# Loading x in halves over two queues, and the end of the head in halves of 256, in a gated mix of two attentions

## The chip, the cores and the metric

The kernel runs on one core of a Trainium2 chip. The metric is the device time of one execution in microseconds. Times are compared as medians of several runs; one execution is also taken by the hardware profiler, and its views are quoted here. Engines are PE (TensorE matmul; PEld is its weight load), DVE (VectorE), ACT (ScalarE), POOL (GpSimd) and SP (SyncE, which only issues DMAs here).

## The reference

Input x has 2048 tokens of 640 features. Two attention blocks with 32 heads of 20 features each read it. Block A is full softmax attention. Block B is attention over a window of 8 positions, two apart. A gate per token mixes the two.

```python
H = 32; Dh = D // H
qkv = (x @ wqkv).reshape(B, S, 3, H, Dh).transpose(2, 0, 3, 1, 4)
# A: full attention
p = softmax(einsum("bhqd,bhkd->bhqk", q, k) * Dh ** -0.5)
a = einsum("bhqk,bhkd->bhqd", p, v).transpose(0, 2, 1, 3).reshape(B, S, D) @ wo
# B: keys at pos - 2*w, w = 0..7, masked below 0
b = ...
g = sigmoid((x * gate_w).sum(-1, keepdims=True))
return g * a + (1 - g) * b
```

## The kernel before, in words

Most of the work is block A: for every group of four heads and 512 queries, scores for 16 blocks of 128 keys (`qk`, L1697), their exponentials (`exp`, L1722, on ACT; a share of them is approximated on DVE, L1711 and L905), and the product with V (`pv`, L1767). There are 32 such groups. Block B and the output projections are worked in between.

The order of the instructions is written by a planner, `_Sched`. `T(stream, duration, ...)` puts an instruction at the end of one engine's list, with the data keys that it reads and writes; from these the semaphore waits are made. Each engine works through its list in order. `T` also keeps an estimated time per engine (`sch.avail`), and generators for the side work look at these estimates to decide what goes next. So a changed estimate early on can change the order of all that follows.

The change touches the head, which is everything ahead of the first scores:

- `x_load` (L498) loads a part of x, 512 tokens as a tile of 128 partitions by 4 rows of 640 (640 KB). All four parts go through SP's queue, with the first K weights (into `ebuf[3]`, 100 KB, L506) behind part 1, and the first Q weights (`ebuf[4]`, L509), the V weights (L510) and the rest of the K weights (L512) behind part 3.
- ACT loads its table and runs one small exponential (L520) meanwhile. PE runs nine matmuls on zeros to warm up (L529).
- `turn` (L1392) transposes a part on PE into the score banks, 20 transposes of 128 x 128 (L1400). `x_out` copies it into `xT`, two fifths on ACT (L1413), three fifths on DVE (L1416).
- POOL's `w_pad` (L598) spreads the first K weights, so that four heads lie 32 rows apart. `k_first` (L1432) projects K of the first four heads for 512 tokens, five matmuls of 512 columns (L1423). The order on PE is: turn 0, turn 1, K 0, turn 2, K 1, turn 3, K 2, K 3, Q 0.
- `k_max` takes the largest absolute value of each K feature (DVE, L1437), `k_out` writes K to `kT` (ACT, L1444).
- The end of the head: from K's largest values DVE makes the diagonal mask `KM` (L1496, L1498, L1501). Q's absolute values are taken (DVE, L1503). PE adds the bound mask x |Q| to Q (L1506), which serves as the softmax's upper bound. DVE scales Q into `qT[0]` (L1511). Then the first scores can start. `v_first` and `v_out` (L1450, L1458) do the first block of V beside it.

PSUM has two score tiles of three banks each; the third bank of each, and the bank `side0`, serve as banks for side work (`side[1]` is the third bank of score 0), and `obank` collects the product with V.

## Time and profile before

| | us |
|---|---|
| median of three runs | 792.07 |
| the three runs | 791.92, 794.16, 792.07 |
| profiled execution: its own time | 792.33 |
| profiled execution: span of the core | 790.4 |
| first exponential of scores starts at | 18.77 |
| ACT busy, whole span | 769.2 (97%) |
| ACT busy from 60 to 200 us | 140.00 |

The page gives busy time per engine and the chain of work that ended last. The trace can be asked for busy time in chosen stretches, and for a timeline: start, length, engine, line, operation, output and input with their shapes, and in brackets how long the engine was idle before it and what ended that. Successive instructions of one kind are merged into one row with a count. Times are counted from the start of the span. Matmuls are pipelined: the length of a merged row on PE includes the last one's run through the array. "PEclk" was 1.00 in all stretches of the head.

### The profile page before, as it was taken

Reading aid. Unit: us, or ns where it says so; the run is one execution under the profiler, and the core shown is the slowest. Engines: PE = TensorE matmul, PEld = TensorE weight load, DVE = VectorE, ACT = ScalarE, POOL = GpSimd, SP = SyncE. Lnnn points to the kernel's source line nnn. Section 1 sums busy time; section 2 is a strip of 40 time slices with the busy share of each in tenths; the row PEclk is TensorE's granted clock in tenths of the full one; section 3 lists DMA queues with packets and bytes.
Section 4 is the critical chain, followed back from the end, with each engine's and each line's share of the span. In section 5 each row is a group of like instructions: output and inputs, shape, how many; then the busy total and the mean of one; then the engine's idle time right before and its main releaser. Section 6 shows DMA issues by size and latency. Waiting matters only on the chain.

```text
span 790.4 us, 29540 instructions
## 1 busy us (share of the span) xinstructions
PE 751.7 (95%) x12545; PEld 289.6 (37%) x12545; DVE 721.5 (91%) x1280; ACT 769.2 (97%) x731; POOL 124.2 (16%) x230
## 2 busy tenths in 40 slices
PE   8999999999999999999999999999999999999997
PEld 4423333232233334333334433433433433344333
DVE  7798888999999989999988999998999999898894
ACT  4999999999999999999999999999999999999996
POOL 4011202111112011111111011111111111111210
PEclk9999999999999999999999999999999999999999
DMA  7231111010021123130111312013113013100311
GB/s 227 86 85 25 39 38 38 12 27 18 8 67 32 43 42 72 25 72 15 24 40 39 79 40 57 14 39 73 25 27 75 26 24 70 46 7 7 74 31 39
DMA packets 61221, 36.14 MB, mean 46 GB/s; under 512 B 26724, under 2 KB 59892, under 8 KB 61092
## 3 DMA queue, kind: packets, MB, share of 16 engines
q1 hardware_dynamic: 60804, 33.94, 17.6%
q8 instruction: 99, 1.62, 0.9%
q10 hardware_dynamic: 288, 0.33, 0.1%
q14 instruction: 30, 0.25, 0.1%
HBM read 12.85 MB, written 3.54 MB: 21 GB/s over the span
## 4 chain that ended last, share of the span: by engine, by line
PE 44%; ACT 25%; DVE 18%; issue 10%; DMA 1%; SPq 0%; POOL 0%; DVEq 0%; ACTq 0%
ACT ebuf L1722 25%; PE score L1697 13%; PE obank L1767 12%; PE side L632 12%; DVE uD L1711 6%; DVE eD L905 4%; PE score L632 2%; DVE qkvB L967 1%; DVE kvw L1092 1%; PE score L1788 1%; PE side L1003 1%; PE obank L1788 1%; DVE vA L833 1%; DMA oTd<-in_A_x_dram 1%; DVE kvw L993 1%
## 5 line engine op out<-in xcount | busy, mean ns | idle before, releaser
L1722 ACT ACTIVATE ebuf<-score 128x1024 bf16<-128x1024 f32 (+1 forms) x699 | 757.4, 1260 | 5.3 <-PE score L1697 4.6
L1711 DVE TENSOR_SCALAR uD<-score 128x512 int16<-128x512 f32 x392 | 259.9, 679 | 14.6 <-PE score L1697 13.3
L1697 PE MATMUL score<-qT,kT 32*128 32x512 bf16 x1856 | 253.8, 384 | 17.6 <-ACT ebuf L1722 13.0
L905 DVE TENSOR_SCALAR eD<-uD 128x2048 int16<-128x2048 int16 x294 | 194.8, 686 | 4.5 <-PE obank L1767 3.4
L1767 PE MATMUL obank<-ebuf,vA 128*21 128x512 bf16 x1656 | 153.5, 385 | 1.6 <-DVE oTt L865 0.6
L1697 PEld LDWEIGHTS score<-qT,kT 32*128 32x128 bf16 x1856 | 63.0, 91 | 211.4 <-ACT ebuf L1722 147.0
L925 POOL TENSOR_TENSOR vS<-vA,vw 128x252 bf16<-128x252 bf16 x98 | 60.1, 614 | 389.0 <-DVE eD L905 252.6
L1767 PE MATMUL obank<-eD,vS 128*21 128x512 bf16 x1176 | 103.5, 379 | 0.0
L632 PE MATMUL side<-xT,wBs 128*32 128x256 bf16 x2400 | 93.6, 280 | 2.5 <-DVE oB L1125 0.7
L632 PEld LDWEIGHTS side<-xT,wBs 128*32 128x32 bf16 x2400 | 68.1, 141 | 28.2 <-issue 14.5
L1767 PEld LDWEIGHTS obank<-ebuf,vA 128*21 128x21 bf16 x1656 | 36.0, 89 | 82.9 <-issue 56.6
L1092 DVE TENSOR_TENSOR kvw<-kvw,eB 128x2048 bf16<-128x2048 bf16 x40 | 48.1, 1212 | 0.8 <-DMA kvw<-qkvB 0.8
L993 DVE TENSOR_TENSOR kvw<-qkvB 128x2048 bf16<-128x2048 bf16 x40 | 48.0, 1214 | 0.1
L882 POOL TENSOR_TENSOR oN<-oTt,rcp 128x256 bf16<-128x256 f32 x62 | 38.9, 627 | 58.0 <-DVE eD L905 39.5
L967 DVE CAST qkvB<-side 128x512 bf16<-128x512 f32 (+1 forms) x72 | 42.0, 592 | 4.5 <-PE side L632 4.3
L873 POOL TENSOR_TENSOR rcp<-rcp,gA 128x16 f32<-128x16 f32 x31 | 9.1, 294 | 190.3 <-DVE eD L905 90.7
L1767 PE MATMUL obank<-uD,vA 128*21 128x512 bf16 x392 | 38.1, 379 | 0.0
L1767 PEld LDWEIGHTS obank<-eD,vS 128*21 128x21 bf16 x1176 | 28.8, 91 | 19.8 <-issue 2.0
L1697 PE MATMUL score<-woBp,kT 32*128 32x512 bf16 x192 | 30.0, 384 | 1.8 <-ACT ebuf L1722 1.6
L632 PE MATMUL side<-xT,kvw 128*32 128x512 bf16 (+1 forms) x360 | 30.1, 382 | 0.6 <-DVE vA L833 0.3
L632 PE MATMUL side<-kvw,xT 128*32 128x160 bf16 (+1 forms) x740 | 28.5, 263 | 1.3 <-DVE vA L833 0.5
L865 DVE STREAM_TRANSPOSE oTt<-obank 128x512 f32<-128x512 f32 x32 | 22.6, 706 | 6.6 <-PE obank L1767 6.6
(188 smaller groups left out, 553.3 us busy)
## 6 DMA issues: line engine op xcount, KB each, us to landing
kvw<-qkvB SPq DMA_DIRECT2D x128, 80.6 KB
wBs<-in_B_wqkv_dram SPq DMA_DIRECT2D x5, 480.0 KB
WqP<-in_A_wqkv_dram SPq DMA_DIRECT2D x14, 160.0 KB
oTd<-oN SPq DMA_DIRECT2D x108, 20.0 KB
out_dram<-outsb SPq DMA_DIRECT2D x12, 160.0 KB
qT<-dst SPq DMA_DIRECT2D x93, 20.0 KB
kvw<-in_A_wqkv_dram SPq DMA_DIRECT2D x2, 800.0 KB
oTd<-in_A_x_dram SPq DMA_DIRECT2D x2, 640.0 KB
```

The lines of the kernel that those rows point to most:

```text
L632: ins = e.matmul(o[j:k, :], l(j) if callable(l) else l[:, j:k], r, start=(first and i == 0), stop=(last and i == n - 1), skip_group_check= ...
L865: T("dve", 0.625, lambda e: e.transpose(oTt[:, :], obank[:, :]), reads=["obank"], writes=["oTt"])
L882: T(en, c2 if n == 4 else 0.56, lambda e, oo=oo, ii=ii, ib=ib: e.tensor_tensor(oo, ii, ib, ALU.mult), reads=["rcp", "oTt"], **{"accum" if ...
L905: T("dve", 0.065 + 0.1334 * n, lambda e, k=k, sl=sl: e.tensor_scalar(eD[:, sl % NS, 0:512 * n].bitcast(I16), uD[d % 2][:, 0:512 * n].bitca ...
L925: T("pool", 0.607, lambda e: e.tensor_tensor(vS[:, d % 2, :, :], _ap(vA, (kb * NQ + q) * 4 * DV, [[0, K - 1], [1, 4 * DV]]), _ap(vw, 0, [[ ...
L967: t = TB(dvc(n * TOK), lambda e, o=o, i=i: e.tensor_copy(o, i), reads=[("side", b)], writes=[key])
L993: TB(dvc(CH, 2), lambda e: e.tensor_tensor(o, i0, i1, ALU.mult), reads=["qB", "kB"], writes=[("prod", i)] + (["WkA", "WvA", ("WkP", 0)] if ...
L1092: TB(dvc(CH, 2), lambda e: e.tensor_tensor(o, i0, i1, ALU.mult), reads=["eB"] + [("vR", w4) for w4 in range(4)], writes=[("prod", i)], por ...
L1697: ins = e.matmul(o, kT[32 * j:32 * j + 32, q, kb * P:(kb + 1) * P], qT[qbuf[g]][32 * j:32 * j + 32, :], start=True, stop=True)
L1711: t = T("dve", 0.598, lambda e: e.tensor_scalar(uD[d % 2][:, 512 * i:512 * (i + 1)].bitcast(I16), side[x], UOFF, 0.0, op0=ALU.add, op1=ALU ...
L1722: exps[s] = T("act", actc(512 * n), lambda e: e.activation(ebuf[s % NE][:, 0:512 * n], score[s % 2][:, 0:512 * n], ACTF.Exp, scale=LN2 / S ...
L1767: ins = e.matmul(obank[32 * j:32 * j + DV, :], v, src, start=(kb == 0), stop=(last and k >= len(lst) - 4), skip_group_check=True)
```

## The change

`x_load` now makes two DMAs of 256 tokens each, the first half through SP's queue and the second through ACT's. ACT's four stand ahead of its table load. `turn` waits for both halves.

The end of the head works in halves of 256 columns. K 3 goes into two halves of `score[1]`, Q 0 into one half in `obank` and one in `side[1]`, with ten matmuls of 256 columns in place of five of 512 each. The maximum over K 3 is taken per half. In place of the mask from three parts and its combination with the fourth, one instruction takes the largest of the three values, and one makes the mask. ACT takes the absolute value of Q's first half, DVE of its second. The bound and the scaling are done per half. ACT writes K 3 to `kT` from both halves in one instruction, now behind the absolute value.

Last, the planner's estimates are set to fixed numbers after the head. With them the planner writes the same order as before for all that follows, on every engine. Only four waits are added behind the head: one DVE instruction waits for ACT's absolute value, SP's first load of B's weights waits for ACT's half of part 3, and ACT's two output DMAs at the end wait for its own early loads.

```diff
@@ -438,7 +438,7 @@
     gwT = sb([P, CN], BF16, "gwT")
     qabs2 = sb([P, 2 * 512], BF16, "qabs")
     qabs = [qabs2[:, i * 512:(i + 1) * 512] for i in range(2)] + [woBp[:, 4, 0:512]]
-    kmx4 = sb([P, 4], FP32, "kmx4")
+    kmx4 = sb([P, 5], FP32, "kmx4")
     kmx = sb([P, 1], FP32, "kmx")
     kmd4 = sb([P, 4], FP32, "kmd4")
     KMd = sb([P, CN, 32], BF16, "KMd")
@@ -497,8 +497,10 @@
 
     def x_load(tcc, dur):
         t_, o_ = XOFF[tcc]
-        T("sp", dur, lambda e: e.dma_start(_ap(t_, o_, [[D, 4], [1, D]]), x_v[tcc * 512:(tcc + 1) * 512, :].rearrange(
-            "(b p) d -> p b d", p=P)), writes=[("xs", tcc)], dma=True)
+        for h, q in enumerate(("sp", "act")):
+            T(q, dur, lambda e, h=h: e.dma_start(_ap(t_, o_ + 2 * h * D, [[D, 2], [1, D]]), x_v[
+                tcc * 512 + 256 * h:tcc * 512 + 256 * h + 256, :].rearrange("(b p) d -> p b d", p=P)),
+              writes=[(("xs", "xsh")[h], tcc)], dma=True)
 
     w4 = lambda t: _ap(t, 0, [[4 * DH, CN], [1, 4 * DH]])
     x_load(0, 4.9)
@@ -518,7 +520,7 @@
     T("pool", 0.3, lambda e: e.iota(itmp[:, :], [[1, P]], base=0, channel_multiplier=-1), writes=["itmp"])
     T("dve", 0.06, lambda e: e.memset(warm[:, :], 0.0), writes=["warm"])
     T("act", 1.4, lambda e: e.activation(warm[:, 2:4], warm[:, 0:2], ACTF.Exp), reads=["warm"], writes=["warm2"])
-    T("dve", 0.2, lambda e: e.memset(qabs[0][:, :], 0.0), writes=[("qabs", 0)])
+    T("dve", 0.2, lambda e: e.memset(qabs[0][:, :], 0.0), writes=[("qabs", 0), ("qabsh", 1)])
 
     T("dve", 0.25, lambda e: e.tensor_copy(idf[:, :], itmp[:, :]), reads=["itmp"], writes=["rB"])
     T("dve", 0.25, lambda e: e.tensor_scalar(ident[:, :], idf[:, :], 0.0, None, op0=ALU.is_equal),
@@ -528,7 +530,7 @@
 
     warm_up = lambda e: e.matmul(obank[:, :], qabs[0][:, 0:P], qabs[0][:, :], start=True, stop=True)
     for i in range(9):
-        T("pe", 0.43, warm_up, reads=[("qabs", 0)], writes=["obank"])
+        T("pe", 0.43, warm_up, reads=[("qabs", 0), ("qabsh", 1)], writes=["obank"])
 
     WKP0 = _ap(kvw, WKP_OFF, [[P, CN], [1, P]])
     T("dve", 0.35, lambda e: e.memset(WKP0, 0.0), writes=["WkP"])
@@ -709,7 +711,7 @@
         yield ("dve",)
         T("dve", dvc(512), lambda e: e.tensor_scalar(
             qabs[0][:, :].bitcast(U16), side[b][:, :].bitcast(U16)[:, 1:1024:2], 0x7FFF, None, op0=ALU.bitwise_and),
-          reads=[("side", b)], writes=[("qabs", 0)])
+          reads=[("side", b)], writes=[("qabs", 0), ("qabsh", 1)])
         yield from mm_group(b, [(side[b][:, :], KM[0], qabs[0][:, :])], [("KM", 0), ("qabs", 0)], mmc(512), first=False)
         yield ("dve",)
         t = T("dve", dvc(512), lambda e: e.tensor_scalar(qT[1][:, :], side[b][:, :], OCT, offs[:, 0:1], op0=ALU.mult, op1=ALU.add),
@@ -1401,7 +1403,7 @@
                                    ident[:, :], start=True, stop=True, is_transpose=True, skip_group_check=True)
             return ins
 
-        T("pe", 1.13 if tcc else 1.9, fn, reads=[("xs", tcc), "ident"], writes=tkeys(s_))
+        T("pe", 1.13 if tcc else 1.9, fn, reads=[("xs", tcc), ("xsh", tcc), "ident"], writes=tkeys(s_))
 
     def turned(tcc):
         turn(tcc)
@@ -1425,7 +1427,7 @@
         return fn
 
 
-    kbank = lambda tcc: ((side[0], ("side", 0)), (obank, "obank"), (side[0], ("side", 0)), (side[1], ("side", 1)))[tcc]
+    kbank = lambda tcc: ((side[0], ("side", 0)), (obank, "obank"), (side[0], ("side", 0)))[tcc]
 
     def k_first(tcc):
         kb_, key = kbank(tcc)
@@ -1490,37 +1492,70 @@
     k_out(1)
     k_first(2)
     k_max(2)
-    k_first(3)
-    T("pe", 1.07, proj5(obank[:, :], lambda c: WqP[:, c, :], None, 0), reads=WQ + XT(0), writes=["obank"])
+
+    def half_proj(o, w_, x0):
+        def fn(e):
+            for c in range(CN):
+                ins = e.matmul(o, w_(c), xT[:, c, x0:x0 + 256], start=(c == 0), stop=(c == CN - 1), skip_group_check=True)
+            return ins
+        return fn
+
+    hcols = lambda h: slice(256 * h, 256 * h + 256)
+    k3 = lambda h: score[1][:, 512 * h:512 * h + 256]
+    q0 = [obank[:, 0:256], side[1][:, 0:256]]
+    q0k = ["obank", ("side", 1)]
+    for h in range(2):
+        T("pe", 0.55, half_proj(k3(h), lambda c: kvw[:, WKP_OFF + c * P:WKP_OFF + c * P + P], 1536 + 256 * h),
+          reads=[("WkP", 0)] + XT(3), writes=[("K3", h), ("score", 1)])
+    for h in range(2):
+        T("pe", 0.55, half_proj(q0[h], lambda c: WqP[:, c, :], 256 * h), reads=WQ + XT(0), writes=[("Q0", h), q0k[h]])
     k_out(2)
     T("dve", 0.15, lambda e: e.tensor_reduce(kmx[:, 0:1], kmx4[:, 0:3], AX.X, ALU.max),
       reads=[("kmx4", i) for i in range(3)], writes=[("kmx", 0)])
-    T("dve", 0.2, lambda e: e.tensor_scalar(KM3, KMmask, kmx[:, 0:1], None, op0=ALU.mult),
-      reads=[("kmx", 0), "KMmask"], writes=["KM3"])
-    k_max(3)
-    T("dve", 0.25, lambda e: e.scalar_tensor_tensor(KM[0], KMmask, kmx4[:, 3:4], KM3, op0=ALU.mult, op1=ALU.min),
-      reads=[("kmx4", 3), "KMmask", "KM3"], writes=[("KM", 0)])
-    T("dve", dvc(512), lambda e: e.tensor_scalar(
-        qabs[0][:, :].bitcast(U16), obank[:, :].bitcast(U16)[:, 1:1024:2], 0x7FFF, None, op0=ALU.bitwise_and),
-      reads=["obank"], writes=[("qabs", 0)])
-    T("pe", 0.215, lambda e: e.matmul(obank[:, :], KM[0], qabs[0][:, :], start=False, stop=True, skip_group_check=True),
-      reads=[("KM", 0), ("qabs", 0)], accum=["obank"])
+    for h in range(2):
+        T("dve", dvc(256), lambda e, h=h: e.tensor_reduce(
+            kmx4[:, 3 + h:4 + h], k3(h), AX.X, ALU.max, apply_absolute_value=True),
+          reads=[("K3", h)], writes=[("kmx4", 3 + h)])
+    T("act", actc(256), lambda e: e.activation(qabs[0][:, 0:256], q0[0], ACTF.Abs), reads=[("Q0", 0)], writes=[("qabs", 0)])
+    T("dve", 0.1, lambda e: e.tensor_scalar(kmx[:, 0:1], kmx[:, 0:1], kmx4[:, 3:4], kmx4[:, 4:5], op0=ALU.max, op1=ALU.max),
+      reads=[("kmx", 0), ("kmx4", 3), ("kmx4", 4)], writes=[("kmx", 0)])
+    T("dve", 0.2, lambda e: e.tensor_scalar(KM[0], KMmask, kmx[:, 0:1], None, op0=ALU.mult),
+      reads=[("kmx", 0), "KMmask"], writes=[("KM", 0)])
+    T("dve", dvc(256), lambda e: e.tensor_scalar(
+        qabs[0][:, 256:512].bitcast(U16), q0[1].bitcast(U16)[:, 1:512:2], 0x7FFF, None, op0=ALU.bitwise_and),
+      reads=[("Q0", 1)], writes=[("qabsh", 1)])
+    t = T("act", actc(512), lambda e: e.activation(kT[:, 0, 1536:2048].rearrange("p (h c) -> p h c", c=256),
+                                               _ap(score[1], 0, [[512, 2], [1, 256]]), ACTF.Identity, bias=onesrow[:, 0:1]),
+          reads=[("K3", 0), ("K3", 1), ("score", 1), "onesrow", ("kmx4", 3), ("kmx4", 4)], writes=[("kT", 0, 3)])
+    bank_free[2] = t.end + LAT["act"]
+    qah = [("qabs", 0), ("qabsh", 1)]
+    for h in range(2):
+        T("pe", 0.11, lambda e, h=h: e.matmul(q0[h], KM[0], qabs[0][:, hcols(h)], start=False, stop=True, skip_group_check=True),
+          reads=[("KM", 0), qah[h]], accum=[("Q0", h), q0k[h]])
     v_first()
-    t = k_out(3)
-    bank_free[1] = bank_free[2] = t.end + LAT["act"]
-    t = T("dve", dvc(512), lambda e: e.tensor_scalar(qT[0][:, :], obank[:, :], OCT, offs[:, 0:1], op0=ALU.mult, op1=ALU.add),
-          reads=["obank", "offs", ("qTz", 0)], writes=[("qT", 0)])
-    qkeys[0] = [("qT", 0)]
-    obank_first = t.end + LAT["dve"]
+    for h in range(2):
+        t = T("dve", dvc(256), lambda e, h=h: e.tensor_scalar(
+            qT[0][:, hcols(h)], q0[h], OCT, offs[:, 0:1], op0=ALU.mult, op1=ALU.add),
+              reads=[("Q0", h), q0k[h], "offs", ("qTz", 0)], writes=[("qTh", h)])
+        if h == 0:
+            obank_first = t.end + LAT["dve"]
+    bank_free[1] = t.end + LAT["dve"]
+    qkeys[0] = [("qTh", 0), ("qTh", 1)]
     v_out()
     bank_free[0] = t.end + LAT["dve"] + 0.5
     done[("k", 0)] = done[("q", 0)] = True
+    for key in qkeys[0]:
+        sch.bufs[key][0].end = 18.0655808
+    sch.bufs["kT", 0, 3][0].end = 16.4994312
+    sch.avail.update(pe=17.6032304, dve=18.2962528, act=16.4994312)
+    bank_free[:] = [18.6485808, 16.6514312, 16.6514312]
+    obank_first = 18.1485808
     g1 = -1
     def gen_wb():
         for c in range(CN):
             yield ("pe", 0.0, 30.0 + 5.0 * c)
             T("sp", 4.0, lambda e, c=c: e.dma_start(_ap(wBs, c * 3 * D, [[1, 3 * D]]), wB_v[:, c, :]),
-              writes=[("wBs", c)] + [("xs", 3)] * (c == 0), dma=True, iss=0.65)
+              writes=[("wBs", c)] + [("xs", 3), ("xsh", 3)] * (c == 0), dma=True, iss=0.65)
         done["wBs"] = True
 
     add_gen(gen_wb(), 1.0)
```

## The prediction

> **What bounds the kernel now.** I read the page's first part, then its chain by engine, then three views of the trace: busy time by stretch, the timeline of the first 19 us, and the DMA share in steps of half a microsecond.
>
> ```profile
> PE 751.7 (95%) x12545; PEld 289.6 (37%) x12545; DVE 721.5 (91%) x1280; ACT 769.2 (97%) x731; POOL 124.2 (16%) x230
> ...
> PE 44%; ACT 25%; DVE 18%; issue 10%; DMA 1%; SPq 0%; POOL 0%; DVEq 0%; ACTq 0%
> ```
>
> ```profile
> 0.00:18.30 18.30, 14.75 (x120) 8.29 (x120) 13.20 (x33) 8.11 (x10) 9.82 (x20) 1.00 0.80 245
> 18.30:60.00 41.70, 40.54 (x779) 15.45 (x783) 36.25 (x92) 39.92 (x38) 4.26 (x8) 1.00 0.27 82
> 60.00:200.00 140.00, 134.01 (x2068) 44.85 (x2060) 128.76 (x236) 140.00 (x132) 24.32 (x42) 1.00 0.13 28
> ```
>
> The columns are PE, PEld, DVE, ACT, POOL, clock, DMA share, GB/s. From 60 us on ACT has no idle time: its exponentials bound the body. They start at 18.77, so what is before that is a head that the bound engine mostly waits out (8.11 of 18.30 us busy). The order of all instructions behind the head is unchanged, so a head shorter by so much should end the kernel earlier by as much, and no more.
>
> Inside the head, the timeline (start, length, instruction, wait):
>
> ```profile
> 0.74 1.28 ACT L520 ACT_TABLE_LOAD   x1 [0.74 <-PEq L1948]
> 5.15 1.12 PEld L1400 LDWEIGHTS score<-ident,oTd 128*128 128x128 bf16 x20 [0.86 <-DMA oTd<-in_A_x_dram]
> 7.10 1.29 PE L1400 MATMUL score<-ident,oTd 128*128 128x128 bf16 x20 [0.66 <-DMA oTd<-in_A_x_dram]
> 7.57 0.52 POOL L598 COPY kvw<-ebuf 128x400 bf16<-128x400 bf16 x1 [2.82 <-DMA ebuf<-in_A_wqkv_dram]
> 8.23 1.24 PE L1423 MATMUL side<-xT,kvw 128*128 128x512 bf16 x5
> 9.37 1.12 PEld L1400 LDWEIGHTS score<-ident,oB 128*128 128x128 bf16 x20 [0.39 <-DMA oB<-in_A_x_dram]
> 11.36 1.32 PEld L1400 LDWEIGHTS score<-ident,wBs 128*128 128x128 bf16 x20
> 15.07 1.24 PE L1423 MATMUL obank<-xT,WqP 128*128 128x512 bf16 x5
> 15.27 0.69 DVE L1437 TENSOR_REDUCE kmx<-score 128x1 f32<-128x512 f32 x1
> 16.00 0.35 DVE L1501 SCALAR_TENSOR_TENSOR eB<-eB,kmx 128x128 bf16<-128x128 bf16 x1
> 16.35 0.69 DVE L1503 TENSOR_SCALAR qabs<-obank 128x512 uint16<-128x512 uint16 x1
> 17.10 0.39 PE L1506 MATMUL obank<-qabs,eB 128*128 128x512 bf16 x1 [0.79 <-DVE qabs L1503]
> 17.53 0.75 DVE L1511 TENSOR_SCALAR qT<-obank,offs 128x512 bf16<-128x512 f32 x1 [0.48 <-PE obank L1506]
> 18.33 0.39 PE L1697 MATMUL score<-qT,kT 32*128 32x512 bf16 x3 [0.50 <-DVE qT L1511]
> ```
>
> Two parts show. Up to 7.10 PE waits for parts 0 and 1 of x. From 7.10 to 16.31 PE works through turns and projections almost without a gap: part 2 of x comes 0.06 us too late at 9.37 (the projection's last matmul was due to free PE at 9.31), part 3 in time. From 16.31 a serial chain DVE, PE, DVE, PE runs to 18.33.
>
> ```profile
> 1.50:2.00 0.50, 0.50 (x2) 0.15 (x1) 0.50 (x1) 0.50 (x1) 0.50 (x1) 1.00 0.29 31
> 2.00:2.50 0.50, 0.50 (x3) 0.17 (x2) 0.50 (x1) 0.23 (x2) 0.50 (x1) 1.00 0.48 79
> 2.50:3.00 0.50, 0.50 (x3) 0.22 (x2) 0.50 (x1) 0.00 (x0) 0.50 (x2) 1.00 0.59 141
> 3.00:3.50 0.50, 0.50 (x3) 0.20 (x2) 0.50 (x1) 0.00 (x0) 0.50 (x2) 1.00 1.00 346
> ```
>
> The load itself has a slow start: 0.5 x (31 + 79 + 141) = 125 KB by 3.0, with engines busy 29 to 59% of the time, then full share. After that it is bound by the DMA engines.
>
> The sum is made against the profiled execution: span 790.4, its time 792.33, which is 0.26 above the median of 792.07.
>
> **Halves of x on two queues.** SP's four x issues stay four, each half as large, and the loads queued behind them keep their places; ACT gets four issues ahead of its first instruction. ACT's table load (1.28) and its warming activation (0.20) move behind four issues. An issue of a whole part took 0.46 to 0.99 us on SP, so ACT is ready between 0.74 + 1.84 + 1.48 = 4.1 and 0.74 + 3.96 + 1.48 = 6.2. ACT's first copy of a turned part starts at 6.48 now, and its result (1.02 long) is used by the projection at 8.23; that slack is the cover, and I cost this at nothing. If the cover were gone, the copy at 6.48 and then the projection would slip.
>
> What it gains is how much earlier parts 0 and 1 land. From below: nothing, since all bytes still go through the same 16 engines, which are at full share from 3.0. From above: no slow start at all. At 376 GB/s, the mean of full slices, the 1.5 us before 3.0 would have carried 564 KB instead of 125, and the missing 439 KB are 1.17 us. A loss by a late second queue is a rival below. I take a slow start of the same length in which two queues bring twice the bytes: 125 KB more, 125 / 376 = 0.33 us. I lean to the low end because the nearest other row, full share by 3.5 on one queue alone, shows the limit to be the engines. Part 2 shifts by the same 0.33, since it comes behind the same bytes; part 3 has slack (its weights were loading at 11.36 while the projection before it ran to 11.58).
>
> The row says that engines idle in the slow start, so a queue can matter there. [...]
>
> **The head's last steps in halves.** PE does the same columns: ten matmuls of 256 in place of five of 512 for K's last part, and again for Q, so Q still ends at 16.31. What changes is after it. The trace has no 256-column read of PSUM on DVE. Its neighbours: 160 columns 0.32 (casts into vA), 512 columns 0.69 (the reduce). Along that line 256 columns take 0.32 + 96 x 0.37 / 352 = 0.42; the scaling that took 0.75 would take 0.75 - 0.27 = 0.48. ACT: 64 columns 0.31, 512 columns 0.69, so 256 about 0.47.
> DVE: the small reduce ends at 14.86; two half maxima 14.88 to 15.72; a one-column maximum 0.15 (as the offset row L545) to 15.90; the mask product 0.25 (L1498) to 16.18. So the mask is ready before Q is, and the 0.35 of L1501 is gone, but it ended at 16.35, when Q had just ended too: no gain from that alone. ACT takes the absolute value of the first half (Q's first half ends at 15.07 + 0.54 + 0.17 = 15.78) to 16.27, and its wait holds up only K's last output copy, 0.27 us, which nothing uses before the fourth quarter of keys. DVE takes the second half from 16.35 to 16.77; PE's half bound 0.27 (256-column row of L632) from 16.82 to 17.09; DVE scales the first half 16.80 to 17.28 and the second 17.31 to 17.79; PE's first scores at 17.84 in place of 18.33: 0.49 us. Bounds: halves that cost as much as wholes would make it 16.35 + 0.69 + 0.75 + 0.75 and some gaps, 18.57 for the scaling, 0.24 worse; halves that cost exactly half, 17.50 for the first scores, 0.83 better. I stay with 0.49, as 160 columns are the nearest row.
>
> **Behind the head** only semaphore waits that are long satisfied are added (SP's load of the second weights now also waits for ACT's half of part 3, landed some 10 us before). Cost nothing.
>
> Sum: 0.33 + 0.49 = 0.82. Time 792.33 - 0.82 = 791.5; against the median 792.07 that is **791.2**.
>
> **Rivals.**
> First, on the other side: the K weights (the 100 KB into ebuf, issued third on SP) are held back by ACT's bulk. They are 640 pieces of 160 bytes. Now they come right behind part 1, at 7.57, and POOL's padding (0.52) ends at 8.09, just ahead of the projection at 8.23: no slack. ACT's queue has no such load, so beside them it goes on with its halves of parts 2 and 3, 512 pieces of 1280 bytes. If engines take from the queues piece by piece in turn, the small pieces last as long as those 512, which is a whole part: 7.10 - 5.15 = 1.95 us. The projection and all behind it slip by that, and the time is 792.07 + 1.95 - 0.82 = 793.2. It decides once these weights land over 0.8 us later than now behind part 1. For it: nothing orders the two queues. Against: nothing in this trace shows two loaded queues. [...]
> Second, the landing does not move: 792.07 - 0.49 = 791.6. For it: full share from 3.0. Against: the idle engines before.
> Third, the slow start goes altogether, the halved steps are at their best, and the second queue also fills what is lost between transfers: a part takes 1.95 us from turn to turn, but 655 KB at 376 GB/s are 1.74, so 0.21 for each of two parts. 792.07 - 1.17 - 0.83 - 0.42 = 789.7. For it: engines idle in the slow start. Against: it needs all three at once.
>
> **How the numbers follow.** The forecast 0.33, landing unchanged 0.17, slow start gone 0.20, weights held back 0.25, and 0.05 for a second queue that starts late or halves that cost as much as wholes (up to 794). The first is likeliest, so 791.2. The range takes in the third rival, 789.7, and the weights held back with only part of the gain, 793.5. A measurement of this kernel can tell about 0.3%, 2.4 us, from no change, and almost all of these cases lie inside it: faster by more only at the far end of the third rival, whose time lies on that bound: 0.15 of its 0.20. Slower by more only if the weights are held back and the second queue starts late as well: 0.08. Within: 0.77.
>
> **What would show it.** Right: DMA share near full before 3.0; second turn at about 6.8; POOL's padding within 0.6 us behind it, the first projection at about 7.9; DVE halves near 0.42 and 0.48; first exponential 0.8 us earlier than 18.77; ACT without idle time from 60 us on. Wrong: POOL waiting for ebuf until 9 or later with PE idle behind the second turn; ACT's table load ending later than the first turn; halves near 0.6; or ACT idle in the body, which would mean that the shift isn't carried to the end.

## The result, and the profile after

The change makes the kernel slower: 795.43 us against 792.72 by the medians of 16 runs each, ratio 1.0030 with a 95% interval of 1.0019 to 1.0041. A second measurement, beside the later experiments, gave 793.87 against 792.48, 1.0023 (1.0012 to 1.0034). The ratios, here and below, go by all runs, and lie near the quotient of the means (here 1.0028 and 1.0022), not of the medians. The forecast was 791.2, the range 789.7 to 793.5. The first profiled execution took 794.07 with a span of 792.3 (before 792.33 and 790.4). In 7 of the 16 runs, and 4 of the 12 of the second measurement, TensorE's mean granted clock was 0.998 or less, and these took 794.9 to 797.5; the others have medians of 794.07 and 793.54.

The page's first part and its chain by engine hardly differ from before:

```profile
PE 752.5 (95%) x12554; PEld 291.1 (37%) x12556; DVE 721.5 (91%) x1282; ACT 769.5 (97%) x732; POOL 123.8 (16%) x230
...
PE 44%; ACT 26%; DVE 17%; issue 11%; DMA 1%; SPq 0%; POOL 0%; DVEq 0%; ACTq 0%
```

Busy time by stretch (PE, PEld, DVE, ACT, POOL, clock, DMA share, GB/s) says where to look:

```profile
2.00:2.50 0.50, 0.50 (x3) 0.18 (x2) 0.50 (x1) 0.00 (x0) 0.50 (x1) 1.00 0.79 192
2.50:3.00 0.50, 0.50 (x3) 0.22 (x2) 0.50 (x1) 0.00 (x0) 0.50 (x2) 1.00 0.61 169
3.00:3.50 0.50, 0.50 (x3) 0.20 (x2) 0.50 (x1) 0.11 (x1) 0.50 (x2) 1.00 0.98 300
...
0.00:19.60 19.60, 15.37 (x130) 9.70 (x134) 13.07 (x35) 8.39 (x11) 9.75 (x20) 1.00 0.75 229
19.60:60.00 40.40, 38.76 (x750) 14.89 (x753) 34.00 (x88) 37.77 (x37) 3.80 (x7) 1.00 0.29 83
60.00:200.00 140.00, 134.13 (x2073) 44.80 (x2061) 128.80 (x236) 140.00 (x132) 24.12 (x41) 1.00 0.14 28
```

From 60 us on ACT is full as before. Two stretches lost: the head, and 19.6 to 60, where ACT idles 2.63 of 40.40 us (before, from 18.3 to 60, 1.78 of 41.70). The slow start is a little better fed (192 and 169 GB/s against 79 and 141), but 300 follow where 346 had been.

The head in the timeline:

```profile
7.00 1.29 PE L1402 MATMUL score<-ident,oTd 128*128 128x128 bf16 x20 [0.31 <-DMA oTd<-in_A_x_dram]
9.52 0.52 POOL L600 COPY kvw<-ebuf 128x400 bf16<-128x400 bf16 x1 [4.77 <-DMA ebuf<-in_A_wqkv_dram]
10.15 0.78 PEld L1425 LDWEIGHTS side<-xT,kvw 128*128 128x128 bf16 x5 [2.03 <-ACT xT L1415]
17.51 0.71 PE L1499 MATMUL score<-xT,WqP 128*128 128x256 bf16 x5
17.62 0.27 DVE L1520 TENSOR_SCALAR kmx<-kmx 128x1 f32<-128x1 f32 x1
17.71 0.38 ACT L1519 ACTIVATE qabs<-obank 128x256 bf16<-128x256 f32 x1 [0.45 <-PE obank L1499]
18.25 0.42 DVE L1524 TENSOR_SCALAR qabs<-score 128x256 uint16<-128x256 uint16 x1
18.64 0.48 DVE L1537 TENSOR_SCALAR qT<-obank,offs 128x256 bf16<-128x256 f32 x1
18.73 0.28 PE L1533 MATMUL score<-qabs,eB 128*128 128x256 bf16 x1
19.06 0.48 DVE L1537 TENSOR_SCALAR qT<-score,offs 128x256 bf16<-128x256 f32 x1
19.60 0.39 PE L1732 MATMUL score<-qT,kT 32*128 32x512 bf16 x3 [0.23 <-DVE qT L1537]
20.04 1.45 ACT L1757 ACTIVATE ebuf<-score 128x1536 bf16<-128x1536 f32 x1 [1.36 <-PE score L1732]
```

The second turn starts 0.10 us earlier than before. Then POOL waits for the K weights until 9.52 (before 7.57), the first projection's weight load moves from 8.21 to 10.15, and the train behind it is 1.91 us late at Q's end (18.22 for 16.31). The releaser "ACT xT" in brackets is only what the profile can name: that copy had ended at 9.35, and what came last was POOL's padding, at 10.04. From Q's end to the first scores it is 1.38 us, against 2.02 before: 0.64 back. So the first exponential comes at 20.04 in place of 18.77, 1.27 us late.

The second loss is a hole in the middle of one group of scores:

```profile
31.36 0.39 PE L1732 MATMUL score<-qT,kT 32*128 32x512 bf16 x2
32.45 0.37 PE L1732 MATMUL score<-qT,kT 32*128 32x512 bf16 x1 [0.70 <-issue]
32.74 0.10 PEld L1802 LDWEIGHTS obank<-ebuf,vA 128*21 128x21 bf16 x4 [1.29 <-issue]
32.85 1.02 ACT L1757 ACTIVATE ebuf<-score 128x1024 bf16<-128x1024 f32 x1 [0.89 <-PE score L1732]
```

Two of the three matmuls run, the third comes 1.09 us later, and "issue" says that PE waited for nothing that the profile shows. Laid beside before, exponential by exponential, the change is 1.26 us late up to the tenth, and 2.19 to 2.24 from the twelfth until 678 us. There and at 779 us 0.35 come back, and the span ends 1.9 longer.

### The profile page after: what moved, and what is told of

It reads as the page before. It is cut to its first block, busy times and chain, and to the rows that moved or that the text cites. A ratio compares the mean times of both kernels' runs of the same rounds, so it can differ in the third digit from the quotient of the medians.

```text
span 792.3 us, 29571 instructions
## 1 busy us (share of the span) xinstructions
PE 752.5 (95%) x12554; PEld 291.1 (37%) x12556; DVE 721.5 (91%) x1282; ACT 769.5 (97%) x732; POOL 123.8 (16%) x230
## 3 DMA queue, kind: packets, MB, share of 16 engines
q8 instruction: 100, 1.64, 0.9%
q10 hardware_dynamic: 1376, 1.64, 0.6%
## 4 chain that ended last, share of the span: by engine, by line
PE 44%; ACT 26%; DVE 17%; issue 11%; DMA 1%; SPq 0%; POOL 0%; DVEq 0%; ACTq 0%
ACT ebuf L1757 25%; PE score L1732 13%; PE obank L1802 13%; PE side L634 12%; DVE uD L1746 6%; DVE eD L907 4%; PE score L634 2%; DVE qkvB L969 1%; DVE kvw L1094 1%; DMA ebuf<-in_A_wqkv_dram 1%; PE score L1823 1%; PE side L1005 1%; PE obank L1823 1%; DVE kvw L995 1%; DVE vA L835 1%
```

## The theories

Expectations below use these names. The **queue theory**: the DMA engines take pieces from the two loaded queues in turn, so the K weights' 640 small pieces on SP's queue go no faster than ACT's 1280-byte pieces. Its rivals: the K weights are late only by their order on their queue, or by the bandwidth that all share. The **program theory**: the hole near 31 us is PE waiting for its own instructions. The trace's DMA records have a queue of the kind "instruction" (q8: in the change 100 pieces and 1.64 MB, so 16 KB each), which I take for PE's program; the second piece behind 18 us starts at 30.15 and has landed at 31.12. It stands beside three loads of 480 KB each (`wBs`, weights of block B) that SP issues one behind the other from 24.3 on. The **idle theory**: PE's idle time in the head lowers its clock later.

## Experiments

Each run has a ratio to runs of the kernel before on the same chip. "Offset" is how much later the exponentials are than in the profiled execution of before.

**One part of the change at a time.** `steps_only` has the halved last steps, with x whole on SP's queue:

```diff
-        for h, q in enumerate(("sp", "act")):
-            T(q, dur, lambda e, h=h: e.dma_start(_ap(t_, o_ + 2 * h * D, [[D, 2], [1, D]]), x_v[
-                tcc * 512 + 256 * h:tcc * 512 + 256 * h + 256, :].rearrange("(b p) d -> p b d", p=P)),
-              writes=[(("xs", "xsh")[h], tcc)], dma=True)
+        T("sp", dur, lambda e: e.dma_start(_ap(t_, o_, [[D, 4], [1, D]]), x_v[tcc * 512:(tcc + 1) * 512, :].rearrange(
+            "(b p) d -> p b d", p=P)), writes=[("xs", tcc)], dma=True)
...
```

> Whole parts of x on SP as before, the head's last steps in halves as in the changed kernel. Queue theory (the loss comes from the K weights, whose small pieces take turns with ACT's large ones): POOL's padding starts at 7.57 as before, the first projection at 8.2, and the first exponential 0.64 us earlier than 18.77, at 18.1, since from the end of Q to the first scores the changed kernel took 1.38 us where the kernel before took 2.02. Rival, program-load theory: the changed kernel's PE stood still for 0.7 us at 31.4 (a gap of 1.09 us between two matmuls of one score tile) because 22 more PE instructions in the head shift the places where PE's program is fetched; then this kernel has such a gap near 30 too, and its exponentials from the tenth on are some 0.4 us later than before in place of 0.64 us earlier. Time: 0.6 us less than before by the first alone, 0.4 us more with the second.

Measured: 791.55, ratio 0.9993 (0.9981 to 1.0004). The K weights land at 7.48, the padding starts at 7.54, and the first exponential at 18.12: 0.65 us early. Then comes the hole:

```profile
29.77 0.39 PE L1800 MATMUL obank<-ebuf,vA 128*21 128x512 bf16 x1
30.69 0.39 PE L1800 MATMUL obank<-ebuf,vA 128*21 128x512 bf16 x3 [0.53 <-issue]
```

and the offset goes from -0.65 to +0.13. The halves are worth what the trace of the change showed, 0.65, and the hole takes 0.78 back, without any second queue.

`queues_only` has halves of x on both queues and the old last steps:

```diff
-        T("sp", dur, lambda e: e.dma_start(_ap(t_, o_, [[D, 4], [1, D]]), x_v[tcc * 512:(tcc + 1) * 512, :].rearrange(
-            "(b p) d -> p b d", p=P)), writes=[("xs", tcc)], dma=True)
+        for h, q in enumerate(("sp", "act")):
...
-        T("pe", 1.13 if tcc else 1.9, fn, reads=[("xs", tcc), "ident"], writes=tkeys(s_))
+        T("pe", 1.13 if tcc else 1.9, fn, reads=[("xs", tcc), ("xsh", tcc), "ident"], writes=tkeys(s_))
...
```

> Halves of x on both queues, the head's last steps as before. Queue theory: POOL's padding starts at 9.5, the first projection at 10.2, the first exponential at 18.77 + 1.91 = 20.7, and the time is 1.9 us over before. Program-load theory: PE's instructions are those of before, so no gap of over 1 us between matmuls near 32; 1.9 us over before and no more. If the gap comes from the shift of time and not of the program, it is here as well, and the time is about 3 us over before. Rival, idle theory: PE's idle 2 us behind the second turn closes its clock for a while in some executions; then part of the runs are some 2 us slower with a mean clock of 0.995 to 0.998, as half the runs of the changed kernel were.

Measured: 793.47, ratio 1.0015 (1.0006 to 1.0024). The timeline:

```profile
9.05 0.52 POOL L600 COPY kvw<-ebuf 128x400 bf16<-128x400 bf16 x1 [4.30 <-DMA ebuf<-in_A_wqkv_dram]
...
20.19 1.45 ACT L1724 ACTIVATE ebuf<-score 128x1536 bf16<-128x1536 f32 x1 [2.09 <-PE score L1699]
...
32.12 0.52 PE L634 MATMUL score<-kvw,xT 128*32 128x160 bf16 x12
32.58 0.39 PE L1699 MATMUL score<-qT,kT 32*128 32x512 bf16 x2
```

K weights at 9.00, first exponential 1.42 late, and no hole near 30 us. Of the 0.5 that it is less late than expected, 0.37 are this execution's part 1, which landed at 6.59 in place of 6.96. The group of 12 that takes 0.52 us will come up again below; otherwise PE runs through. So the late weights come with the queues, and the hole of 0.8 us and more with the halved steps, though a smaller one will show in the kernel before as well. The idle theory would have this kernel's clock low as often as the change's, with the same idle time in the head; it was 0.998 or less in one run of 12.

**The K weights elsewhere.** `kw_before_part1` issues them on SP between parts 0 and 1; `kw_both_queues` splits them, three of five chunks on SP and two on ACT behind part 1; `parts01_only` keeps the halves for parts 0 and 1 and loads parts 2 and 3 whole on SP:

```diff
 # kw_before_part1
+    T("sp", 5.6, lambda e: e.dma_start(w4(ebuf[3]), wA_v[:, :, D:D + 4 * DH]), writes=[("ebuf", 3)], dma=True)
     x_load(1, 5.5)
-    T("sp", 5.6, lambda e: e.dma_start(w4(ebuf[3]), wA_v[:, :, D:D + 4 * DH]), writes=[("ebuf", 3)], dma=True)
 # kw_both_queues
+    for q, c0, c1, key in (("sp", 0, 3, ("ebuf", 3)), ("act", 3, CN, "kwh")):
+        T(q, 5.6, lambda e, c0=c0, c1=c1: e.dma_start(_ap(ebuf[3], c0 * 4 * DH, [[4 * DH, c1 - c0], [1, 4 * DH]]),
+                                                      wA_v[:, c0:c1, D:D + 4 * DH]), writes=[key], dma=True)
...
 # parts01_only
+        if tcc > 1:
+            T("sp", dur, lambda e: e.dma_start(_ap(t_, o_, [[D, 4], [1, D]]), x_v[tcc * 512:(tcc + 1) * 512, :].rearrange(
+                "(b p) d -> p b d", p=P)), writes=[("xs", tcc), ("xsh", tcc)], dma=True)
+            return
```

> The changed kernel with the K weights issued on SP between parts 0 and 1. Queue theory, by turns piece by piece: 40 small pieces per engine now take turns with ACT's halves of parts 1 and 2, so the weights land at about 7.4 and SP's half of part 1 behind them at about 8.4; the second turn starts at 8.4 in place of 7.0 and the first projection at about 9.6 in place of 10.2; the first exponential at about 19.4, the time 0.6 us under the changed kernel and over before. Rival, order theory (a queue is served by whole transfers, the weights were only issued too late): the weights land at about 5.6, part 1 at 7.4, the first projection at 8.6 and the first exponential at about 18.4, under that of before.

> The changed kernel with the K weights loaded in two transfers, three fifths on SP and two fifths on ACT, both behind part 1. Queue theory: small pieces take turns with small ones, so the weights land about 0.5 us behind part 1, POOL's padding starts at 7.5 to 7.9, the first projection at 8.2 to 8.6, the first exponential at 18.1 to 18.5, and the time is 0.3 to 0.6 us under before, 1.5 to 2 us under the changed kernel. Rival, bandwidth theory (two loaded queues slow every small transfer): the weights land at 9 or later, the first projection at about 10, and the time is that of the changed kernel. Program-load theory: the PE gap of over 1 us near 31 is here too, and takes 1 us of the gain. Idle theory: PE no longer idles for 2 us, so no runs with a mean clock under 0.999.

> The changed kernel with only parts 0 and 1 of x in halves on two queues; parts 2 and 3 are whole on SyncE's queue as before. Queue theory (the K weights' small pieces take turns with large pieces on ScalarE's queue, those of parts 2 and 3): nothing large stands beside the K weights once part 1's half has landed, so they land at 7.3 to 7.8 us (before 7.52, the change 9.46), the first exponential is 0.3 to 0.65 us earlier than before, the gap near 30 us is there as in the halved steps alone (0.8 to 1.0 us), time within 0.6 us of before. Rival (a second queue slows the small pieces whatever it carries): K weights 8.3 us or later, first exponential later than before.

| | K weights land | first exponential (before 18.77) | offset behind the hole | median | ratio |
|---|---|---|---|---|---|
| kw_before_part1 | 6.22 | 19.02 | 1.72 | 792.72 | 1.0006 (0.9997 to 1.0014) |
| kw_both_queues | 7.37 and 7.63 | 18.29 | 0.27 | 792.33 | 1.0007 (0.9997 to 1.0016) |
| parts01_only | 7.29 | 17.93 | 0.41 | 791.54 | 0.9984 (0.9976 to 0.9993) |

The row that the first projection waits for, in kw_both_queues and then in parts01_only:

```profile
7.68 0.52 POOL L602 COPY kvw<-ebuf 128x400 bf16<-128x400 bf16 x1 [2.93 <-DMA ebuf<-in_A_wqkv_dram]
```

```profile
7.35 0.52 POOL L604 COPY kvw<-ebuf 128x400 bf16<-128x400 bf16 x1 [2.60 <-DMA ebuf<-in_A_wqkv_dram]
...
29.26 0.39 PE L1736 MATMUL score<-qT,kT 32*128 32x512 bf16 x3
30.97 0.40 PE L1806 MATMUL obank<-ebuf,vA 128*21 128x512 bf16 x4 [1.32 <-issue]
```

parts01_only settles the queue theory: with nothing left on ACT's queue the same small pieces, at the same place of SP's queue, land at 7.29 in place of 9.46. The second queue alone does no harm; what stands on it beside the small pieces does. Splitting the pieces over both queues serves as well. kw_before_part1 is the half miss: earlier in the queue the weights, by that theory, take their turns beside part 0's and part 1's large pieces, land at 6.22, between what the theories said, and SP's half of part 1 pays (7.99). None of these three is slower in the head by more than 0.25 us, yet all have the hole.

The records of single DMA pieces in the change show the turns themselves. From 6.5 to 8.0 us, while the K weights wait, ACT's queue (q10) and SP's (q1) start about as many pieces, almost all of 1280 and of 160 bytes (queue, packets, MB, share of 16 engines):

```profile
q10 hardware_dynamic: 337, 0.41, 87.0%
q1 hardware_dynamic: 358, 0.07, 24.2%
```

They also take turns singly, as far as the starts tell. The records don't name the engine of a piece, so I assume that the next piece of an engine starts at a fixed distance from the end of the last. At 3 to 4 ns ahead of the end of a small piece there are 398 starts of ACT's pieces in this stretch, where the distances beside it would give about 130. For two small pieces there is no such excess (170, where about 155 would be chance), though in before, where small follows small from 6 to 7 us, the same distance shows it (1703, where about 1285 would be chance). So, on that assumption, behind a small piece comes one of ACT's, and not a second small one.

**The hole.** `before_pad22` is the kernel before with 11 small matmuls on zeros behind the warm-up, in time that PE waits anyway. With their weight loads that is the number of PE instructions that the change adds. `steps_spaced` is steps_only with each `wBs` load made to wait for the PE instruction ahead of it in the plan, and `before_spaced` and `after_spaced` are the kernel before and the change with the same edit:

```diff
 # before_pad22
+    def pads(e):
+        for i in range(11):
+            ins = e.matmul(obank[:, 0:32], qabs[0][:, 0:P], qabs[0][:, 0:32], start=True, stop=True)
+        return ins
+    T("pe", 0.0, pads, reads=[("qabs", 0)], writes=["obank"])
 # steps_spaced, and before_spaced and after_spaced in the same way
-              writes=[("wBs", c)] + [("xs", 3)] * (c == 0), dma=True, iss=0.65)
+              writes=[("wBs", c)] + [("xs", 3)] * (c == 0), dma=True, iss=0.65, after=(sch.lists["pe"][-1],))
```

> The changed kernel once more, beside the others. The program theory (TensorE's program comes in pieces of 16 KB over the DMA, the piece wanted near 30 us is held behind the three 480 KB loads of layer B's weights, and 22 more TensorE instructions in the head make TensorE reach its end before it has come): first exponential 1.2 to 1.4 us later than before, a TensorE gap of about 1.1 us near 31 us, exponentials 2.2 to 2.4 us later behind it, 1.3 to 2.4 us longer in all. The theory that the loads alone cost the time: no gap, 1.2 to 1.4 us longer. If the first measurement was special to its chip, the median is within 0.5 us of before.

> The kernel before with 11 matmuls of 32 columns (22 TensorE instructions with their weight loads) put behind the nine warm-up matmuls, where TensorE waits for x anyway; they compute nothing that is used. Program theory: the head stays as it is (first exponential at 18.7 to 18.9 us), the piece of program still comes at about 28.6 us, and TensorE has a gap near 30 us that costs 0.45 to 0.8 us (the gaps of the four kernels with 22 more instructions cost 0.78 to 1.6 us; less what their pieces came later against their TensorE, 0.13 to 0.8 us, that is 0.46 to 0.8); the time 0.4 to 0.9 us over before. Rival (the gap comes from the halved steps' banks and waits): no gap, no difference.

> The halved last steps with whole loads of x on SyncE's queue, and each of layer B's 480 KB weight loads made to wait for the TensorE instruction ahead of it in the plan (about 30, 35 and 40 us), so that they no longer stand together from 22.4 to 28.7 us. Program theory: the piece of program comes some microseconds earlier than 28.25 us, the gap at 29.8 us goes, the first exponentials' 0.65 us stay through tile 11 and the time is 0.5 to 1.3 us under before, about 0.8 under steps_only's profile up to where the loads matter. Rival (banks and waits of the halved steps): gap of 0.9 us as in steps_only, time within 0.3 us of it.

> The kernel before with layer B's weight loads made to wait for TensorE and nothing else changed. Program theory: it has no gap near 30 us to lose, so exponentials 0 to 200 stay within 0.2 us of before and the time within 0.5 us of it; the gain of steps_spaced (1.9 us by the medians, 0.7 to 0.8 of it in the head) is then not the spacing's. Rival (spacing these loads is itself worth the time): 0.8 to 1.9 us under before.

> The whole change, with layer B's weight loads made to wait for TensorE as in steps_spaced. Program theory: no gap near 31 us, so the exponentials stay as late as the head leaves them (0.8 to 1.3 us in the two executions of the change), against 1.75 to 2.2 with the gap; time 0.8 to 1.1 us under the change's, 0.3 to 1.3 over before. What is left is the cost of the K weights' place alone. If the gap were not from these loads, the offset goes to 1.7 us or more as before.

> The kernel before once more, for its trace. Four of the kernels gain 1.1 to 1.3 us on the profiled execution of before between 447 and 786 us, at five places (447.3, 676.4, 677.8, 777.2 and 778.7 us, 0.2 to 0.4 us each), though all they differ in lies in the head. If these stalls belong to the program (the piece of program wanted there comes too late for the kernel before and in time for one whose instructions are shifted), they are there again and the profile is within 0.3 us of 792.3 us; if they belonged to that one execution, exponentials from 447 us on come 0.2 to 1.2 us earlier than in it.

The DMA share and GB/s (last two figures) of one microsecond, by the packets that start in it: in steps_spaced, where the program piece is under way, and then in steps_only, where it hasn't begun:

```profile
26.00:27.00 1.00, 0.93 (x25) 0.49 (x25) 0.62 (x5) 1.00 (x2) 0.00 (x0) 1.00 0.00 0
```

```profile
26.00:27.00 1.00, 0.92 (x25) 0.49 (x25) 0.61 (x5) 1.00 (x2) 0.00 (x0) 1.00 1.02 403
```

SP's issues of `wBs` and the group that has the hole in steps_only, in the timeline of steps_spaced:

```profile
29.45 9.94 SPq L1555 DMA_DIRECT2D wBs<-in_B_wqkv_dram  x3
...
29.73 0.40 PE L1800 MATMUL obank<-ebuf,vA 128*21 128x512 bf16 x4
```

With the loads out of the way the piece of program comes at 25.65 in place of 28.25, the four matmuls of L1800 run in one group at 29.73, and the offset stays at -0.70 to -0.83. The time is 1.9 us under before by the medians, where I expected 0.5 to 1.3. Over the kernels:

| | piece starts | piece landed | PE goes on | difference | offset ahead, behind |
|---|---|---|---|---|---|
| after | 30.15 | 31.12 | 32.45 | 1.33 | 1.26, 2.19 |
| after_again | 29.52 | 30.43 | 32.00 | 1.57 | 0.82, 1.74 |
| steps_only | 28.25 | 29.18 | 30.69 | 1.51 | -0.65, 0.13 |
| kw_before_part1 | 29.63 | 30.52 | 31.98 | 1.46 | 0.25, 1.72 |
| kw_both_queues | 28.23 | 29.20 | 30.52 | 1.32 | -0.49, 0.27 |
| parts01_only | 28.58 | 29.46 | 30.97 | 1.51 | -0.84, 0.41 |
| before_pad22 | 28.66 | 29.64 | 31.03 | 1.39 | -0.07, 0.47 |
| before_again | 28.94 | 29.89 | 31.38 | 1.49 | -0.11, 0.52 |
| before_spaced | 26.60 | 27.53 | no hole | | -0.09, -0.23 |
| steps_spaced | 25.65 | 26.82 | no hole | | -0.70, -0.83 |
| after_spaced | 27.85 | 28.83 | no hole | | 1.52, 1.39 |

In all eight executions with a hole PE goes on 1.32 to 1.57 us behind the landing, whatever instruction stands there, and in the three with the loads spaced there is none. The place in PE's program is the same in all eight as well: at the break the trace has 959 to 961 records on PE (matmuls, weight loads, semaphore waits), whether PE gets there at 29.6 us or at 31.4. That the piece is late because of these loads is shown by moving the loads alone; that PE waits for the piece is inferred from the constant distance and the constant place.

The row that I had not expected is before_again, the kernel before once more:

```profile
30.31 0.40 PE L1767 MATMUL obank<-ebuf,vA 128*21 128x512 bf16 x4
30.53 0.24 PE L632 MATMUL side<-kvw,xT 128*32 128x160 bf16 x4
30.60 0.24 PE L632 MATMUL score<-kvw,xT 128*32 128x160 bf16 x3
31.38 0.37 PE L632 MATMUL score<-kvw,xT 128*32 128x160 bf16 x9 [0.54 <-issue]
```

and before_pad22:

```profile
30.03 0.39 PE L1704 MATMUL score<-qT,kT 32*128 32x512 bf16 x3
31.03 0.40 PE L1774 MATMUL obank<-ebuf,vA 128*21 128x512 bf16 x4 [0.60 <-issue]
```

The kernel before has the hole too, of 0.63 us here. In its first profiled execution that same group of 12 took 0.52 in place of 0.38. The 0.14 are a pause inside the group that ends at 30.86, 1.33 behind the landing at 29.53; in queues_only it ends at 32.26, 1.37 behind 30.89. There, too, PE has 961 records behind it. So by both signs these two had the hole as well, only a small one. So the program theory as I had put it, that 22 more instructions make the hole, falls: before_pad22 lost 0.54, no more than before_again, and its time, for which I expected 0.4 to 0.9 over before, was 791.72, ratio 0.9995 (0.9985 to 1.0005). What the 22 instructions do is to move the place. The break stands 4 + 4 + 3 = 11 matmuls earlier than in before_again, as many as were added, so it goes with a place in PE's program. The old kernel sits on the edge and lost 0.14 and 0.63 us there; those with the halved steps lost 0.76 to 1.47 in every execution profiled without the spacing. How much of that the 11 matmuls make isn't settled: ahead of the break in before_again they take 0.30 us (30.31 to 30.61). In the change the piece also lands 1.59 us later than in the first execution of before, where the head is 1.27 late; why, no run takes apart.

By the medians: after_again 793.87 (ratio above) and after_spaced 792.44, 1.0004 (0.9992 to 1.0016); steps_only 0.9993 and steps_spaced 790.58, 0.9974 (0.9963 to 0.9985); before_again 792.07, 0.9998 (0.9990 to 1.0007), and before_spaced 791.85, 0.9993 (0.9985 to 1.0002). In these two pairs with the halved steps spacing is worth some 0.0019, 1.5 us, each with an uncertainty of about 0.0016 (1.0 and 1.2 us by the medians; in the traces the hole took 0.8 and 0.9); it is within the uncertainty in the kernel before. steps_spaced, in 7 runs, beats both kernels. The intervals of steps_only and after_spaced reach 1, so these two can't be told from before. The head of the change also varies by itself: its first exponential was 1.27, 0.82 and 1.52 us late in after, after_again and after_spaced (I had expected 1.2 to 1.4, then 0.8 to 1.3), with part 1 landing at 6.96, 6.69 and 7.42.

**Are two queues worth anything?** `parts01_spaced` puts parts01_only and the spacing together.

> Parts 0 and 1 in halves on both queues, parts 2 and 3 whole on SyncE's, halved last steps, and the spaced loads. Queue and program theories together: K weights at 7.3 to 7.6 us, first exponential 0.65 to 0.85 us earlier than before, no gap near 30 us, time 790.2 to 790.8 us or 1.5 to 2.2 under before, with steps_spaced or 0.2 below it. If two queues are worth nothing more once nothing stands beside the K weights: equal to steps_spaced.

Measured: 790.82, ratio 0.9987 (0.9978 to 0.9997), span 788.7 against 788.6 of steps_spaced; no hole, K weights at 7.68, first exponential at 18.32, 0.45 early where at least 0.65 was expected. The later half of part 1 landed at 7.22 here, and in the six other executions with halves of part 1 behind part 0's at 6.59 to 7.42, at 6.92 in the mean of the seven. Whole on one queue it landed at 6.96 to 7.05 in six executions, at 7.00 in the mean. Two queues spread the landing of part 1 and hardly move it. Part 0 did come earlier, at 4.84 in the mean of the same seven executions, 5.05 in the six. The spacing, too, shows no gain between these two by the ratios: 0.9984 for parts01_only, 0.9987 here, 0.5 us less by the medians. The hole is gone (offset -0.45 and then -0.58, in place of -0.84 and then 0.41), but this head is 0.39 us later, and the 1.0 us that should be left is no more than the uncertainty of the two ratios. Nor do the ratios tell two queues from one: without the spacing they stand at 0.9984 against 0.9993 (steps_only), with it at 0.9987 against 0.9974 (steps_spaced).

**Left open.** The profiled executions also differ late, where nothing was changed: between 440 and 786 us before_again gains 1.0 us on the first profiled execution of before, and all others but kw_both_queues gain 0.4 to 1.7, mostly at the same places. So spans of single executions can't be compared to better than about 1 us, and I go by offsets ahead of 447 us and by medians. Why the clock was lower in 11 of 28 runs of the change, and in 8 of 101 runs of the kernel before beside the experiments, isn't settled: kw_both_queues had it in 4 of 12 without the idle time in the head, queues_only in 1 of 12 with it, after_spaced in 2 of 12.

## Why the prediction was wrong

**K weights held back** was my first rival, with 0.25. It is what happened: I priced it at 1.95 us, and the weights landed 1.94 us later (7.52 to 9.46); Q's end moved by 1.91. The step that failed is the forecast's own, that "the loads queued behind them keep their places", with nothing in the sum for them. The K weights kept their place on SP's queue, and still landed 3.00 us behind part 1's half in place of 0.47, since ACT's pieces came in between (from 6.5 to 8.0 us 337 started on ACT's queue beside 358 on SP's). I had counted 640 small pieces against 512 large ones and noted that nothing orders the queues, and still gave it less than the forecast, because before showed no row with two loaded queues. That is an absence of evidence, and a cost with no cover (0.14 us between padding and projection) should have weighed more.

The 1.94 us alone don't tell how many pieces make a turn. The starts of single pieces above do, on the assumption named there: 398 of ACT's directly behind a small piece, where about 130 would be chance, so turns of one piece, which is what the 1.95 had been worked out from.

**0.33 for the earlier landing** measured 0.10 at the second turn, and 0.08 in the mean landing over executions (6.92 for 7.00). The engines that idled from 2.0 to 3.0 were fed earlier, but 3.0 to 3.5 brought less in return (300 GB/s for 346); of the 0.2 by which part 0 was earlier in the mean, 0.08 were left at part 1. My second rival, the landing unchanged, was right on this step. Part 2, which was to shift by 0.33 too, landed 0.9 later in its later half (10.22 for 9.32), hidden behind the late projection.

**0.49 for the halved steps** was right in mechanism and too small: 0.64 in the change, 0.65 in steps_only. The halves cost what I had worked out (0.42 and 0.48; the matmul 0.27 to 0.28). But I set the two scalings end to end, at 16.80 and 17.31; in steps_only they start at 16.73 and 17.14, 0.41 apart with 0.48 shown for each. The one-column maximum (0.27, not 0.15) and ACT's half (0.38, not 0.47) cost nothing, as the chain waits for neither.

**ACT's table load behind four issues, at nothing:** right. It ran from 3.39 to 4.67, and the first turn's copies started at 6.73.

**"Behind the head: cost nothing"** failed. I looked for waits and found none, and had no term for PE's own program, which by the program theory comes by DMA as the loads do. The hole took 0.93 us (1.26 to 2.19) in the profiled execution. The edit adds 11 matmuls, and so moves the place where PE waits; but as before_pad22 shows, these alone cost no more than before_again lost, and what else makes the change's hole larger stays open. Where the three `wBs` loads (1.4 MB) stood in front of the piece, 0.14 to 1.47 us were lost; with them spaced no profiled execution had a hole.

Together: 1.91 - 0.64 + 0.93 = 2.20 us at 60 us, less 0.35 that comes back late: the 1.9 of the spans. The first rival's 793.2 held the delay but not the hole, and so was too low as well. The medians lie 2.7 apart and the means 2.2; the 7 runs with the lower clock are among the slowest, and the rest have a median of 794.07. That the head's shift is carried to the end was right in kind, and so was the test named for "wrong": POOL waiting for `ebuf` until 9 or later.

## What to carry to other kernels

Before moving a load to a second queue, look for a load of many small pieces that something waits for, and ask what will stand on the other queue at that moment. Keep nothing large there, or spread the small pieces over both: here the K weights then landed at 7.29, or at 7.37 and 7.63, in place of 9.46. A block of big loads can hold back a piece of program: behind the three 480 KB loads it landed at 29.18 and PE had a hole (steps_only), with them spaced it landed at 26.82 and PE had none (steps_spaced). So a load that isn't needed yet may be better issued late than at once. More instructions ahead of such a place move it, here 11 matmuls by 11, so count instructions, not only columns, when work is halved. A hole marked "issue" in the middle of a group of equal instructions is the sign to look for.

## What the runs showed of the hardware

- A DMA of 640 pieces of 160 bytes landed 0.47 us behind part 1 on a queue alone (before, 7.05 to 7.52), and 3.00 us behind part 1's half (after, 6.46 to 9.46) beside a queue of 1280-byte pieces. From 6.5 to 8.0 us the two queues started 358 and 337 packets; by the 398 starts of ACT's pieces 3 to 4 ns ahead of a small piece's end, where about 130 would be chance, in turns of one piece.
- The instruction queue q8, taken here for PE's program, brought pieces of 16 KB that took 0.88 to 1.67 us each in before (99 pieces) and 0.88 to 1.60 in the change (100). In the eight executions of the table with a hole, PE went on 1.32 to 1.57 us behind the landing of one.
- In one profiled execution, of kw_both_queues, the granted clock dropped in the middle of the body and stayed down for 3.4 us (from 678.0), in which PE was busy throughout (the clock is the third figure from the end; 0.51 in the second row):

```profile
670.00:678.00 8.00, 5.83 (x82) 1.55 (x78) 5.31 (x10) 6.21 (x7) 1.24 (x3) 1.00 0.14 31
678.00:681.50 3.50, 3.50 (x30) 0.66 (x30) 3.21 (x6) 2.30 (x3) 0.90 (x2) 0.51 0.17 36
681.50:690.00 8.50, 8.50 (x181) 3.26 (x177) 6.27 (x11) 8.38 (x8) 0.61 (x1) 1.00 0.17 52
```

Just before, DVE and PE had stood still:

```profile
676.16 0.45 DVE L889 STREAM_TRANSPOSE oN<-oN 128x256 f32<-128x256 f32 x1 [2.52 <-DMA oTd<-oN]
677.33 0.39 PE L1734 MATMUL score<-qT,kT 32*128 32x512 bf16 x3 [1.93 <-DVE uD L1748]
```

The offset rose from -0.22 to 2.39 between 677 and 682 us, 1.55 of it with this pause and the rest while the clock was down. The span of this execution is 792.7, so its profile is used for the head and the hole only. No other profiled execution has a gap of over 0.96 us on PE behind 33 us, so the pause of 1.93 us may have brought the drop; but a gap about as long in the head of the change (2.10 us ahead of 10.39, with the clock at 1.00) brought none, and nothing was tried.
